# Tap rows by one load, folds evicted in pairs, halved first blocks and last outputs, a new order of pieces

## The chip, the core and the metric

The kernel runs on one core of a Trainium2 chip. A core has a tensor engine (PE, with its weight loads listed as PEld), VectorE (DVE), ScalarE (ACT), GpSimd (POOL) and SyncE (SP), which here issues every DMA. Each engine works through its own queue in order and waits on semaphores for the others. The metric is the device time of the program in microseconds, lower is better; a run gives the time of one whole execution.

## What is computed

Packed attention, then two gated networks, for 8 batches of 576 positions, 8 heads of 64 channels (512 in all):

```python
p_packed = sm_attn(p, k, v)              # 32 packed queries per head
out = sm_attn(q, p_packed, p_packed)     # x = out, heads joined: (8, 576, 512)
gate = sigmoid(conv5(x))                 # causal convolution per channel, 5 taps
val = x @ w_val
x = (gate * val) @ w_out
h = relu(x @ w_in)                       # 1024 wide
u, v = h[..., :512], h[..., 512:]
v_s = w_spatial @ layernorm(v) + b_spatial
return (u * v_s) @ w_out2
```

`w_in`, `w_val`, `w_out`, `w_out2` and the convolution's taps come as 64-bit floats.

## The kernel before

Channels lie on the 128 partitions, positions in the free dimension, so a batch's `x` is four blocks of 128 by 576, worked on in two halves of 288 columns. Products that must keep their precision split both operands into a rounded part `hi` (ScalarE copy) and a rest `lo` (VectorE subtraction), `split` at L137, and take three products of them, `mm3` at L146.

The order of all work is written out by hand: `ORDER` (L21) is a list of tokens, and `run` (L719) advances the generator of each by one step, or by as many as stand behind the dot. `0hv3.2` is two steps of `hv(3)` of batch 0. A step ends at a `yield`, so the list sets each engine's queue. A digit ahead of an attention piece (`sa`, `tr`, `av`, `ppt`, `sb`, `sn`, `sb2`, `m`, `xt`, `cv`) means the batch after it, so that the attention of batch 1 lies among the network of batch 0.

Setup pieces (no digit): `ik`, `ip`, `iv`, `ic` load keys, packed queries, values and taps of batch 0. `ro`, `rw`, `rv`, `ru` (`load_raw`, L583) load a 512-column block of a 64-bit weight, 512 KB; `uo`, `uw`, `uv`, `uu` (`unit`, L588) convert it with `from_f64` (L545): two ScalarE instructions into a temporary, a shift (L554) and an addition (L556) on VectorE. `fv` and `fu` (`fold`, L594) multiply `w_out` with one half of `w_in` into the folded weight `wp`: for each of four 128-row parts `m` four matmuls over `k` (L601), then a ScalarE copy and a VectorE subtraction of 512 columns (L608, L610). Two parts share one accumulator tile. `cb` (`tap_rows`, L651) makes the five taps as rows, repeated for each packed query: a selection matrix on GpSimd, a transpose, five matmuls and two ScalarE copies. `ppk` (L257) multiplies them with the packed values, and `cx` (L352) does batch 0's convolution with them on the tensor engine; the later batches do it in `cv` on VectorE.

Pieces of a batch: `sa` scores of the packed queries with row maxima and exponentials, `av` their weighted values, `ppt` a transpose, `sb` the second scores, `sn` and `sb2` their softmax, `m` the packed values times `w_val`, `xt` the attention output; `val` the gated value `g1`, `hv` the layer-normed half, `hu` the other half, `sp` the spatial product `g2`, `out` (L518) the last product: 2 x 12 matmuls into one accumulator, one ScalarE eviction of 576 columns (L535), one store of 288 KB (L537).

Accumulators come from a pool of four tiles of two banks each (`ps2`, L124); work tiles of 576 columns from a pool of eight (`f`, L113): exponentials, `sn` tiles, convolution sums, gated products before their split, and outputs until their store is done.

Of the kernel before, what the change touches and what calls it, by code (L numbers as in the profile page):

```python
# [21 lines left out]
ik0 ip0 ik1 ic0 cw0.3 cb0 rw0 uw0 sa0 cb0 ro0 sa0 cb0 uw0 uo0.2 rw1 uw1 iv1 cb0 sa0 uw0 uo0 fv3 fv2 sa0 uw1.2 ro1
uo1.3 fv0 ru0 fv1 fv2 iv0 cb0 sa0 tr0 av0 tr1 av1 uu0 rw2 av0 lq0 uu0 uw2 av0 av1 uw2 fv1 av1 ppt0 fv3 uw2 lq1 ppt0
ro2 uu0 ru1 rw3 av0 sb0 fv0 av1 sn1 uo2 lp0 uo2 fu0 sn1 uo2 uu1 sn0 rv2 uu1 sn1 uw3 ro3 sn1 uw3 uu1 sn0 fu1 uw3 ru3
sn0 fv3 uo3.2 uv2 uu3 ru2 fv1 uv2 sb21 fu2 fv0 uo3 uu2 rv0 uu3 fv2 fu1 sn0 sb21 wo0 sb20 fu3.2 fu2 lk1 rv3 uu3 fv0 uv2
uv0 uu2 fv2 uu2 sb21 fv1 sb21 sb20 fv1 sb20.2 rv1 fv1 uv1.2 fv3.2 fv0.2 sb21 uv3 fv3 fu0.2 fu3 fu2 fv2.2 fu3.2 fu0 fu3
wo3 uv1 ws0 fu2 uv3 uv0 sb20 uv3 fu2.2 cx1 uv0 ws3 wo0.2 0lp0 0lq1 sb20 cx1 sb21 fu1 wo0 fu1.2 ws4 m0.2 wo3 m0 cx0 wo3
0val0 wo3 fu1 ws3 lv1 ws1 cx0 fu0.2 0val0 ws3 ws2.2 ws4 0val3.2 0val1.2 0val0.2 0val3 0val2.2 0val0 ws1 0val1.2
0val2.2 lk0 0val1 0val3 0val2 0sa0 0val3 0hv0.2 0sa0 0hv0.2 0sa0 0hv1 ws4 wo0 0hv1.2 0hv0 0sa0 0hu0 0tr0 0hv0.2 ws1
0sa0 0tr1 0hv1 0hv2.2 0hv1.2 0hv2.2 wo3 0hu0 lv0 wo1 0av0.2 wo0 2lp0 0av0 0hv2 0av1.2 wo3 ws2 0hv4 ws0 0hv2.2 wo1 0hv1  # L30
wo1 wo2 0hv3 0hu0 0hv4 0hv3 0av1 0hv4 0hu2 0hv3.2 0hv4.2 0ppt0 0hv4 0ppt0 ws0 0hu2.2 0lq0 0sb0 0sn1 0hv3.2 wo1 0hv4
0hv3 0hu3.2 0sn0.2 0hu1.2 ws4.3 wo1 0sn0 0hv4.2 0sn0 ws4 0sn1.2 0sb20.2 0hv4 0sn1 0sb20.3 0sp2 0sp1.2 wo2 0hu3 0sb21.3
0hu1 0sp1.2 0sp2.2 wo2 0sp0.2 0sb21 0xt0 wo2 0sp0 0sb21.2 0sp1 wo2.2 0sb20 0lv1 0xt0 0sp2.2 0m0.2 0xt1 0m0 0sp0.2
0sp3.3 0xt1 0cv3 1val0.2 0sp3 0cv1 wo1 0sp3 0lk0 0out2 1val1.2 0out2 0cv0 0cv2 0out2 0cv1 0cv2 0out0 0out2 0out0.2
0out1 0cv2 0cv0 0out1.2 0cv3 1val2.2 0out3 0cv1 1val1 0out3 0cv0 1val3 1val2 0cv3 1val3 1val2 1val0.3 1val3 1val1.2
0out1 0lk1 0out3 1val2 1val3 1sa0 1val3 1hv2.2 1sa0.3 1tr0 1hv1.2 1hu3.2 1lq1 1hv0 1sa0 1hv1 1tr1 1hv2 1av1 1hv1 1av1
1hu3 0lv0 1hv2 1av0.2 1av1 1hv1.3 2lq0 1av0 1hv2.2 1hu0.2 1lq0 1hv2 1hv0 1hv3 1hv0 1hv4 1hu0 1hv0.2 1hv3 1hv0.2
1ppt0.2 1hv3.2 1hu1 1hv4.3 1sb0 1hv3.2 1hv4 1m0 1sn0 1hv3 1hu1 1sn0.2 1hu1 1hu2.2 1sn1 1m0 1hv4.3 1m0 1hv4.2 1sp0.2
1sn0 1sb20 1sn1.3 1sb21.3 0out0 1sb21 1hu2 1sb20.2 1sp3.2 1lv0 1sb21.2 1sp3.2 1sp2 1sp0.2 1sp3 1sb20.2 1sp1.3 1sb20
1xt0.2 1sp1 1lk1 1sp2 0out3 1sp2.2 1sp0 1xt1.2 1cv0 2val0 1sp1 2val0 1cv3 1sp2 1out2.2 1cv0 1out2.2 1cv2 1cv3 1lv1  # L40
1out0 1out1.2 1cv0 1cv1 1out3 1out0 1cv3 1out1 1out3.2 1cv1 2val0 2val1.2 2val2 1cv2 1cv1 2val1 1lp0 2val2 2val0.2
2val3.2 1cv2 2val2 2val1 1lk0 2val1 1out0.2 2sa0 2val3 2val2.2 2val3 2lq1 2val3 2hv0 2hv3 2hv0 2sa0.2 2hu1.2 2sa0
2hv0.2 2tr0 2sa0 2tr1 2hv3 2hu1 2hv0.2 2hv3 2hv0 2hu0 2hv2 2hv3.2 2av1.2 2hv3 2av0 2hv3 2hv2.3 2av1 2lv1 2av0.2 2hv1
2ppt0 2hv1.2 2ppt0 2hv1 2hu0 2sb0 2hv2 2sn0 2hv4 2hv2.2 2sn1 2hv4.3 2sn0 2hv1.2 2sn1 2hv4.3 2hu0 2hu2.2 2hv4 2sn1 2hv1
2hu2 2hu3.3 2hv4.2 2sp1.2 2sn0.2 2sp1 2sb20 1out1 2sp0.2 2sb20 2sp1 2lv0 2sb20.2 2sp1 2sn1 2sb21.2 2sp2.2 1out3
2sb21.3 2lk1 2sp0.3 2sb20.2 2sp2.2 2lk0 2sp3.3 2sp2 2xt0.2 2sp3.2 2m0.2 2xt1 2sb21 2xt1 2cv0 2m0 2out1 2cv3 2out1 2cv0
2out1 3val2 2cv2 2cv3 2out2 2out0 2cv1 2out2 3val0.2 2out1 2out2.2 2cv1 3val1 2cv2 2cv0 3val0 3lq1 2out0.2 3val2 2cv3
# [24 lines left out]
6cv1 6sp2 6sp1 6cv1 6sp3 6sp2 6sp3.3 7val2 6sp2 6cv2 6sp3 6cv0 7val0.2 7val2 6cv3 6out1.4 6cv1 6cv2.2 6out3.3 7val1.2
6out2 6cv0.2 7val0 6out2 7val2 7val1 6cv3 6out0.2 7val0.2 7val1 6cv3 7val2 7val1 7val3.3 6out0 7val2 7val3.2 7hv3
6out0 7hv3.4 7hv0 7hv3.2 7hv0.2 7hv1.4 7hv4 7hv1.3 7hv0 7hv4 7hu3.2 7hv4.7 7hv0 7hv2 7hu2 7hu3 7hv0 7hv4 7hv2 7hu2.2
7hu1 7hv2 7hu1.2 7hv2.3 7hu0.3 7hv2 7hv0 7sp0.2 7sp2.2 7sp1 7sp2 7sp3 7sp0.3 7sp2.2 6out2 7sp1.2 7sp3.2 7sp1.2 7sp3.2
6out2 6out3 7out1 7out0.3 7out2 7out1.3 7out3.4 7out0 7out2.3
"""


@with_exitstack  # L80
def packed_attention_gated_mlp(
    ctx: ExitStack,
    tc: tile.TileContext,
    qT: bass.AP,
    kT: bass.AP,
    vT: bass.AP,
    pT: bass.AP,
    w_val: bass.AP,
    conv_w: bass.AP,
    w_outT: bass.AP,  # L90
    w_in: bass.AP,
    wsT: bass.AP,
    w_out2: bass.AP,
    outT: bass.AP,
):
# [35 lines left out]
    def f32(t):  # L131
        return t.bitcast(F32)
# [9 lines left out]
    def mms(out, pairs):  # L142
        for i, (a, b) in enumerate(pairs):
            nc.tensor.matmul(out, lhsT=a, rhs=b, start=(i == 0), stop=(i == len(pairs) - 1))  # L144
# [656 lines left out]
```

## Time and profile before

| | us |
|---|---|
| median of three runs | 587.71 (587.62 to 588.37) |
| the profiled execution | 587.61 |
| its span, first to last instruction | 585.8 |
| tensor engine busy | 570.2 (97%) |
| VectorE busy | 442.8 (76%) |
| ScalarE busy | 298.1 (51%) |

A busy share says how long an engine had an instruction running; where the time could be shorter is read from the engine that the end waits for, stretch by stretch: its timeline with the idle time before an instruction and what ended it, the windows of a batch, and the chain of waits, which is followed back from the last instruction.

### The profile page before, as it was taken

How to read it: one execution, taken by the hardware profiler on the slowest of the kernel's cores; microseconds unless marked ns; L12 is line 12 of the kernel's file. 1: busy time of each engine (PE TensorE's matmuls, PEld its weight loads, DVE VectorE, ACT ScalarE, POOL GpSimd, SP SyncE). 2: the span in 40 equal slices, each digit the busy share in tenths (PEclk: the TensorE clock that was granted, in tenths of full speed). 3: DMA queues.
4: the chain of work that ended last, by engine and by line, in shares of the span. 5: the costliest groups of instructions: out<-in, count | busy, mean ns of one | idle time of the engine just before them, and what ended most of it. 6: DMA issues, size and time to landing. Idle time of an engine off the chain costs nothing.

```text
span 585.8 us, 12443 instructions
## 1 busy us (share of the span) xinstructions
PE 570.2 (97%) x5267; PEld 503.1 (86%) x5267; DVE 442.8 (76%) x847; ACT 298.1 (51%) x524; POOL 27.3 (5%) x51
## 2 busy tenths in 40 slices
PE   3998999999999999999999999999999999999997
PEld 2444889898899989898999989898999899998997
DVE  3697899996879867898759866997779968885330
ACT  4678665654435634654436553655446454453321
POOL 2000010000100010001000010001000010001000
PEclk9999999999999999999999999999999999999999
DMA  8965430053203150023300422013500300000012
GB/s 318 409 268 179 152 107 22 1 194 121 62 1 112 62 204 11 21 67 116 97 1 21 168 90 104 19 49 103 190 24 21 102 2 2 1 20 21 1 41 81
DMA packets 16615, 52.55 MB, mean 90 GB/s; under 512 B 1968, under 2 KB 2992, under 8 KB 16560
## 3 DMA queue, kind: packets, MB, share of 16 engines
q1 hardware_dynamic: 16560, 51.77, 25.0%
q8 instruction: 41, 0.67, 0.5%
q14 instruction: 14, 0.11, 0.1%
HBM read 42.32 MB, written 9.44 MB: 88 GB/s over the span
## 4 chain that ended last, share of the span: by engine, by line
PE 93%; DVE 4%; DMA 1%; ACT 1%; issue 0%; SPq 0%; DVEq 0%; ACTq 0%
PE ps L144 82%; PE ps L601 2%; PE ps L238 2%; PE ps L194 2%; PE ps L341 2%; PE ps L273 2%; PE ps L325 1%; DMA kq<-kT 1%; PE ps L360 1%; DVE wp L610 1%; DVE sT L286 0%; DVE sT L306 0%; DVE mx L202 0%; DVE sm L301 0%; DVE raw L556 0%
## 5 line engine op out<-in xcount | busy, mean ns | idle before, releaser
L144 PE MATMUL ps<-ws,vn 128*128 128x288 f32 (+1 forms) x896 | 122.1, 295 | 0.0
L144 PEld LDWEIGHTS ps<-ws,vn 128*128 128x128 f32 (+1 forms) x896 | 119.6, 188 | 2.4 <-issue 1.3
L144 PEld LDWEIGHTS ps<-g,wp 128*128 128x128 f32 x768 | 103.5, 188 | 5.0 <-issue 3.2
L144 PE MATMUL ps<-g,wp 128*128 128x288 f32 x768 | 107.3, 296 | 0.0
L144 PE MATMUL ps<-g,wo 128*128 128x288 f32 x768 | 105.9, 295 | 1.0 <-DVE g L140 1.0
L144 PEld LDWEIGHTS ps<-g,wo 128*128 128x128 f32 x768 | 102.9, 188 | 3.0 <-ACT x L349 1.3
L380 DVE SCALAR_TENSOR_TENSOR acc<-x,cw,acc 128x572 f32<-128x572 f32 (+1 forms) x112 | 90.0, 815 | 4.3 <-ACT acc L376 1.0
L144 PE MATMUL ps<-wp,g 128*128 128x512 f32 x384 | 91.9, 393 | 0.0
L144 PEld LDWEIGHTS ps<-wp,g 128*128 128x128 f32 x384 | 70.8, 188 | 16.5 <-issue 0.7
L138 ACT CAST g<-g 128x576 fp32r<-128x576 f32 x64 | 42.4, 675 | 56.7 <-DVE g L510 40.8
L140 DVE TENSOR_TENSOR g<-g,g 128x576 fp32r<-128x576 f32 x64 | 47.7, 751 | 6.5 <-ACT g L138 5.7
L457 POOL TENSOR_TENSOR rstd<-rstd,mhalf 128x1 f32<-128x1 f32 (+1 forms) x40 | 23.6, 593 | 522.2 <-DVE rstd L455 447.6
L138 ACT CAST vn<-vr 128x512 fp32r<-128x512 f32 (+1 forms) x40 | 24.6, 622 | 45.1 <-DVE vr L459 45.0
L510 DVE TENSOR_TENSOR g<-ps,u 128x576 f32<-128x576 f32 x32 | 23.8, 753 | 27.4 <-PE ps L144 26.9
L535 ACT COPY o<-ps 128x576 f32<-128x576 f32 x32 | 20.3, 635 | 35.7 <-PE ps L144 35.7
L144 PE MATMUL ps<-Ah,Mh 128*128 128x288 f32 x128 | 37.9, 296 | 0.0
L144 PE MATMUL ps<-Ah,Ml 128*128 128x288 f32 x128 | 37.8, 295 | 0.0
L144 PE MATMUL ps<-Al,Mh 128*128 128x288 f32 x128 | 37.8, 295 | 0.0
L439 ACT ACTIVATE vr<-ps 128x512 f32<-128x512 f32 x32 | 19.2, 602 | 34.9 <-PE ps L144 32.3
L140 DVE TENSOR_TENSOR vn<-vr,vn 128x512 fp32r<-128x512 f32 (+1 forms) x40 | 27.0, 684 | 13.1 <-ACT vn L138 12.9
L451 DVE BATCH_NORM_STATS2 st<-vr 128x6 f32<-128x512 f32 (+1 forms) x40 | 27.4, 685 | 11.7 <-ACT vr L439 9.0
L459 DVE TENSOR_SCALAR vr<-vr,mv,rstd 128x512 f32<-128x512 f32 (+1 forms) x40 | 21.2, 536 | 11.9 <-POOL rstd L457 11.8
(108 smaller groups left out, 680.4 us busy)
## 6 DMA issues: line engine op xcount, KB each, us to landing
v<-vT SPq DMA_DIRECT2D x16, 650.0 KB, 5.0
kq<-kT SPq DMA_DIRECT2D x16, 576.0 KB, 4.7
kq<-qT SPq DMA_DIRECT2D x16, 576.0 KB, 4.3
outT<-o SPq DMA_DIRECT2D x32, 288.0 KB, 2.5
raw<-w_in SPq DMA_DIRECT2D x8, 512.0 KB, 10.4
raw<-w_outT SPq DMA_DIRECT2D x4, 512.0 KB, 9.9
raw<-w_val SPq DMA_DIRECT2D x4, 512.0 KB, 10.3
raw<-w_out SPq DMA_DIRECT2D x4, 512.0 KB, 7.6
```

The lines of the kernel that those rows point to most:

```text
L138: nc.scalar.copy(out=hi, in_=src)
L140: nc.vector.tensor_tensor(out=lo, in0=src, in1=f32(hi), op=ALU.subtract)
L144: nc.tensor.matmul(out, lhsT=a, rhs=b, start=(i == 0), stop=(i == len(pairs) - 1))
L194: nc.tensor.matmul(ps[g][NPK * qt:NPK * qt + NPK, h // 2, SQ * (h % 2):SQ * (h % 2) + SQ], lhsT=pT_, rhs=k[:, SQ * qt:SQ * qt + SQ], start ...
L238: nc.tensor.matmul(ps[NPK * h:NPK * h + NPK, :65], lhsT=aT[:, 9 * (h // 2) + 4 * (h % 2) + t, :], rhs=v[:, h, t, :], start=(t == 0), stop= ...
L380: nc.vector.scalar_tensor_tensor(out=acc[:, sft:], in0=x[:, :S - sft], scalar=cw[:, c, tap:tap + 1], in1=acc[:, sft:], op0=ALU.mult, op1=A ...
L439: nc.scalar.activation(out=vr, in_=ps, func=AF.Relu)
L451: nc.vector.bn_stats(st[:w], vr[:w])
L457: nc.gpsimd.tensor_tensor(out=rstd[:w], in0=rstd[:w], in1=mhalf[:w], op=ALU.pow)
L459: nc.vector.tensor_scalar(out=vr[:w], in0=vr[:w], scalar1=mv[:w, 0:1], scalar2=rstd[:w], op0=ALU.subtract, op1=ALU.mult,)
L510: nc.vector.tensor_tensor(out=halves(t), in0=ps[:, :, :SH], in1=halves(self.u.pop(c)), op=ALU.mult)
L535: nc.scalar.copy(out=halves(t), in_=ps[:, :, :SH])
```

## The change

- `ORDER` is a new list for the setup and all batches. The first weights that are loaded and folded are now the `u` half of `w_in` and `w_out`, then the `w` half; taps (`ic`, `cb`) come later.
- `FIRST`: the blocks `o0` and `w0` are loaded and converted in two column halves.
- `fold(j, hf)` takes two parts `m` at once, matmuls alternating between the two banks of one tile, and evicts both with one copy and one subtraction of 1024 columns.
- `tap_rows` loads the rows already repeated (`conv_r`, 128 x 640 values of 64 bit, made by the host) and converts them; the selection matrix, the transpose and the matmuls go.
- In the last batch (`cut`) the matmuls of `hv`, `hu`, `sp` and `out` are cut into steps of three, and `out` evicts and stores each half of 288 columns by itself, with an accumulator of its own for the second.
- `sa` may stop between its head pairs; the dictionaries of loaded tiles are read without removing the entry.

```diff
-ik0 ip0 ik1 ic0 cw0.3 cb0 rw0 uw0 sa0 cb0 ro0 sa0 cb0 uw0 uo0.2 rw1 uw1 iv1 cb0 sa0 uw0 uo0 fv3 fv2 sa0 uw1.2 ro1
...
-6out2 6out3 7out1 7out0.3 7out2 7out1.3 7out3.4 7out0 7out2.3
+ip0 ik0 ik1 ro0 uo0 sa0.4 uo0 ru0 ro0 uu0.3 uo0 fu0 iv0 ru1 iv1 uo0.3 sa0 tr0 sa0 tr1 fu1 av0.2 uu1 av1 uu1 ro1 lq1
+lq0 av0 uu1 fu0 uo1 fu1 uo1 av1.2 uo1 ppt0.2 rw0 uw0 rw0 uw0 fu1 sb0 uw0.2 fu0.2 uw0 fu1 sn0 uw0 sn1 fv1 sn0 rw1 uw1
+rw2 uw1 sn1 uw2 uw1 sn1 uw2 sn0 ro2 uo2 fv0 fv1 uo2 rw3 uw2 sn1 fv0 sb21 fv0 ro3 uo2 sn0 sb20 sb21 fv1.2 uo3.2 fv0 ru2
+uw3.2 sb20 fv1.2 fv0.2 uu2 ic0 uu2 uw3 uo3 fv1 uu2 cb0.3 sb21 ru3 uu3 cb0 uu3 lp0 sb20 fv1.2 av1 av0 uu3 rv0 uv0 fv0.2
+fu1 rv3 uv3 sb20 fv0 rv2 fu1 fv1 sb21 ws2 fv0 uv0 fu1.2 ws4 ws3 fu0.2 uv3 uv2 rv1 uv1 sb20 sb21 wo0 uv1 cx0 uv2 2lp0
+ws1 uv0 lv0 uv1 uv2 uv3 fu1.2 fu0.2 sb21 wo0.2 cx0 lk1 m0 cx1 sb20 m0 wo0 fu0 m0 0val0.2 fu0 0val2.2 ws3.2 cw0.2 cx1
...
+7sp2 7sp3.2 6out2 7sp3.5 7sp1 7out1 7out0 7sp2 7sp1.2 7out0 7sp2 7sp3 7out1 7out0 7out3.2 7out2.2 7sp3 7out2 6out1
+7sp3 7out0 7out1.2 7out2 7out3 7out0 7out3 7out1.3 7out0.2 7out2.2 7out3 7out1.2 7out0.2 7out3 7out2.3 7out3.3
...
+    def mms(out, n, pair, cut=False):
+        for i in range(n):
+            a, b = pair(i)
+            nc.tensor.matmul(out, lhsT=a, rhs=b, start=(i == 0), stop=(i == n - 1))
+            if cut and i % 3 == 2 and i < n - 1:
+                yield
...
+            for n in range(2):
+                if self.cut and n:
+                    ps = ps2.tile([P, 2, 512], F32, tag="ps2", name="ps2")
...
+                if self.cut:
+                    nc.scalar.copy(out=t[:, ss], in_=ps[:, n, :SH])
+                    nc.sync.dma_start(out=dst[:, ss], in_=t[:, ss])
...
+    def parts(kind, k):
+        return [slice(0, DM // 2), slice(DM // 2, DM)] if kind + str(k) in FIRST else [slice(0, DM)]
...
+    def fold(j, hf):
+        ps = ps2.tile([P, 2, 512], F32, tag="ps2", name="ps2")
         hs = slice(hf * DM, (hf + 1) * DM)
         for k in range(NC):
+            for i in range(2):
+                m = 2 * j + i
+                nc.tensor.matmul(
+                    ps[:, i], lhsT=woT[:, k, P * m:P * m + P], rhs=homes["uw"[hf]](k),
+                    start=(k == 0), stop=(k == NC - 1),
+                )
+                yield
...
+        hi, lo = (w[:, 2 * j:2 * j + 2, hs] for w in wp)
+        yield from split(hi, lo, ps)
...
     def tap_rows():
...
+        n = CONV * P
+        block = vn_p.tile([P, 4 * n], I32, tag="vn1", name="taps")
+        raw, tmp = block[:, :2 * n].rearrange("p (n t) -> p n t", t=2), block[:, 2 * n:]
+        nc.sync.dma_start(out=raw, in_=words(conv_r))
+        yield
+        dst = block[:, :n]
+        cwr.append(dst.bitcast(F32).rearrange("p (a b) -> p a b", a=CONV))
+        yield from from_f64(lambda: dst, raw, n, tmp=tmp)
```

## Rows read from the trace of the kernel before

**Rows 1.** From the page: engine totals, then granted clock and traffic in 40 slices.

```profile
PE 570.2 (97%) x5267; PEld 503.1 (86%) x5267; DVE 442.8 (76%) x847; ACT 298.1 (51%) x524; POOL 27.3 (5%) x51
...
PEclk9999999999999999999999999999999999999999
...
GB/s 318 409 268 179 152 107 22 1 194 121 62 1 112 62 204 11 21 67 116 97 1 21 168 90 104 19 49 103 190 24 21 102 2 2 1 20 21 1 41 81
```

**Rows 2.** Windows of two batches: stretch, length, busy time per engine (instructions), clock, DMA.

```profile
195.20:261.52 66.32, 66.32 (x642) 60.54 (x647) 52.22 (x100) 33.33 (x58) 3.21 (x5) 1.00 0.23 79
...
327.88:394.45 66.57, 66.57 (x642) 60.59 (x648) 53.21 (x101) 32.67 (x57) 3.11 (x5) 1.00 0.24 82
```

**Rows 3.** Timeline of the tensor engine, setup: start, length, instruction, idle before and releaser.

```profile
14.04 6.75 PE L601 MATMUL ps<-winv,woT 128*128 128x512 f32 x10 [1.67 <-DVE woT L556]
...
46.67 1.12 PE L601 MATMUL ps<-raw,woT 128*128 128x512 f32 x2 [1.85 <-DVE wp L610]
...
55.86 0.40 PE L144 MATMUL ps<-Ah,Mh 128*128 128x288 f32 x1
```

**Rows 4.** Timeline of the weight loads around the change of their distance.

```profile
17.62 0.34 PEld L601 LDWEIGHTS ps<-winv,woT 128*128 128x128 f32 x1 [0.52 <-issue]
18.47 0.20 PEld L601 LDWEIGHTS ps<-winv,woT 128*128 128x128 f32 x1 [0.52 <-issue]
18.91 0.19 PEld L601 LDWEIGHTS ps<-winv,woT 128*128 128x128 f32 x1 [0.24 <-issue]
```

**Rows 5.** Chain that ended last, pieces of the setup: start, length, what.

```profile
1.64 5.92 DMA kq<-kT
...
20.79 1.29 PE ps L238 x78
...
24.34 1.24 PE ps L273 x32
...
47.79 2.61 PE ps L360 x80
...
52.32 1.02 PE ps L325 x16
```

**Rows 6.** Timeline of the end of the run, all engines.

```profile
567.72 0.69 PE L144 MATMUL ps<-g,wo 128*128 128x288 f32 x4
567.92 0.76 DVE L510 TENSOR_TENSOR g<-ps,u 128x576 f32<-128x576 f32 x1 [1.11 <-PE ps L144]
...
569.40 12.50 PE L144 MATMUL ps<-g,wo 128*128 128x288 f32 x92 [0.99 <-DVE g L140]
...
582.00 0.64 ACT L535 COPY o<-ps 128x576 f32<-128x576 f32 x1 [0.96 <-PE ps L144]
```

**Rows 7.** Timeline of VectorE, setup.

```profile
8.90 1.42 DVE L202 TENSOR_REDUCE mx<-ps 128x4 f32<-128x576 f32 x2 [0.37 <-PE ps L194]
10.36 0.68 DVE L208 COPY m<-mx 32x8 f32<-32x8 f32 x4
...
11.75 0.19 DVE L211 TENSOR_REDUCE m<-m 32x8 f32<-32x32 f32 x1
11.97 0.69 DVE L214 TENSOR_SCALAR nb<-m 32x8 f32<-32x8 f32 x4
...
13.30 0.69 DVE L556 CUSTOM_DVE_ANT_0 woT<-woT,tmp 128x1024 uint16<-128x1024 uint16 x1
13.90 0.42 DVE L554 TENSOR_SCALAR winv<-tmp 128x512 int32<-128x512 int32 x1
...
54.54 1.23 DVE L140 TENSOR_TENSOR Ml<-ps,Mh 128x1024 fp32r<-128x1024 f32 x1 [2.53 <-ACT Mh L138]
...
58.19 0.69 DVE L610 TENSOR_TENSOR wp<-ps,wp 128x512 fp32r<-128x512 f32 x1 [0.65 <-ACT wp L608]
```

**Rows 8.** DMA issues of the last 3.5 us: count, KB each, us to landing.

```profile
outT<-o SPq DMA_DIRECT2D x1, 288.0 KB, 2.1
```

**Rows 9.** Groups by line and form, first 80 us: busy time, mean ns of one.

```profile
L369 ACT ACTIVATE gate<-ps 128x288 f32<-128x288 f32 x8 | 2.6, 422 | 0.0
```

More of the change, by code (lines that the diff above doesn't have):

```diff
@@ L20 @@
 GATE0 = True
+FIRST = ("o0", "w0")
 ORDER = """
[L22 to L25 removed]
@@ L26 @@
[L26 to L35, printed above, removed]
@@ L140, in split, with mm3, pair @@
         nc.vector.tensor_tensor(out=lo, in0=src, in1=f32(hi), op=ALU.subtract)
-    def mms(out, pairs):
-        for i, (a, b) in enumerate(pairs):
-            nc.tensor.matmul(out, lhsT=a, rhs=b, start=(i == 0), stop=(i == len(pairs) - 1))
-    def mm3(out, steps):
-        mms(out, [p for (ah, al), (bh, bl) in steps for p in ((ah, bh), (ah, bl), (al, bh))])
+    def mms(out, n, pair, cut=False):
[4 more added lines that the diff above has]
+                yield
+    def mm3(out, n, step, cut=False):
+        def pair(i):
+            (ah, al), (bh, bl) = step(i // 3)
+            return ((ah, bh), (ah, bl), (al, bh))[i % 3]
+        return mms(out, 3 * n, pair, cut)
     vn = []
@@ L179, in __init__, with scores, head @@
             self.pp = self.ppk = self.x = None
-        def heads(self, lhsT, kind):
-            src = [kq_t.pop((kind, self.b, i)) for i in range(2)]
-            return [ps2.tile([P, 2, 512], F32, tag="ps2", name="ps2") for _ in range(2)], [
-                (g, h, lhsT[64 * g:64 * g + 64, NPK * h:NPK * h + NPK], src[h // 2][64 * g:64 * g + 64, h % 2])
-                for h in range(4)
+        def scores(self):
+            return [ps2.tile([P, 2, 512], F32, tag="ps2", name="ps2") for _ in range(2)]
+        def head(self, lhsT, kind, h):
+            src = kq_t[kind, self.b, h // 2]
+            return [
+                (g, lhsT[64 * g:64 * g + 64, NPK * h:NPK * h + NPK], src[64 * g:64 * g + 64, h % 2])
                 for g in range(2)
@@ L189, in sa @@
         def sa(self, _):
-            ps, heads = self.heads(pbd_t.pop(self.b), "k")
-            for i in range(0, 8, 2):
+            ps = self.scores()
+            for h in range(4):
                 for qt in range(4):
-                    for g, h, pT_, k in heads[i:i + 2]:
+                    for g, pT_, k in self.head(pbd_t[self.b], "k", h):
                         nc.tensor.matmul(
@@ L269, in sb @@
         def sb(self, _):
-            ps, heads = self.heads(self.ppT, "q")
+            ps = self.scores()
             for n in range(2):
-                for g, h, pT_, q in heads:
-                    nc.tensor.matmul(
-                        ps[g][NPK * h:NPK * h + NPK, n, :SH],
-                        lhsT=pT_, rhs=q[:, n * SH:(n + 1) * SH],
-                        start=True, stop=True, tile_position=(64 * g, NPK * h),
-                    )
+                for h in range(4):
+                    for g, pT_, q in self.head(self.ppT, "q", h):
+                        nc.tensor.matmul(
+                            ps[g][NPK * h:NPK * h + NPK, n, :SH],
+                            lhsT=pT_, rhs=q[:, n * SH:(n + 1) * SH],
+                            start=True, stop=True, tile_position=(64 * g, NPK * h),
+                        )
             self.sps = ps
@@ L400, in val @@
                 ss = slice(n * SH, (n + 1) * SH)
-                mm3(
-                    ps[:, n, :SH],
-                    [
-                        ((at.M[0][:, g, cs], at.M[1][:, g, cs]), (at.A[g][0][:, ss], at.A[g][1][:, ss]))
-                        for g in range(2)
-                    ],
+                yield from mm3(
+                    ps[:, n, :SH], 2,
+                    lambda g: ((at.M[0][:, g, cs], at.M[1][:, g, cs]), (at.A[g][0][:, ss], at.A[g][1][:, ss])),
                 )
@@ L432, in hv @@
             w_hi, w_lo = ([w[:, k, DM:] for k in range(NC)] for w in wp)
-            g1 = [self.g1[k] for k in range(NC)]
             ts_ = slice(P * tt, P * tt + w)
             if w == P:
-                mm3(ps, [((g1[k][:, 0, ts_], g1[k][:, 1, ts_]), (w_hi[k], w_lo[k])) for k in range(NC)])
+                yield from mm3(
+                    ps, NC, lambda k: ((self.g1[k][:, 0, ts_], self.g1[k][:, 1, ts_]), (w_hi[k], w_lo[k])), self.cut
+                )
                 yield
@@ L440, in hv @@
             else:
-                mms(ps, [(self.tail[:, k, :], wk) for k in range(NC) for wk in (w_hi[k], w_lo[k])])
+                yield from mms(ps, 2 * NC, lambda i: (self.tail[:, i // 2, :], (w_hi, w_lo)[i % 2][i // 2]))
                 yield
@@ L475, in hu @@
                 ss = slice(n * SH, (n + 1) * SH)
-                mm3(
-                    ps[:, n, :SH],
-                    [
-                        (
-                            (wp[0][:, k, cs], wp[1][:, k, cs]),
-                            (self.g1[k][:, 0, ss], self.g1[k][:, 1, ss]),
-                        )
-                        for k in range(NC)
-                    ],
+                yield from mm3(
+                    ps[:, n, :SH], NC,
+                    lambda k: ((wp[0][:, k, cs], wp[1][:, k, cs]), (self.g1[k][:, 0, ss], self.g1[k][:, 1, ss])),
+                    self.cut,
                 )
@@ L692, in packed_attention_gated_mlp @@
         "uu": lambda k: unit("u", k),
-        "fv": lambda m: fold(m, 1),
-        "fu": lambda m: fold(m, 0),
+        "fv": lambda j: fold(j, 1),
+        "fu": lambda j: fold(j, 0),
         "ws": spatial,
@@ L770, in by_pair @@
         return np.moveaxis(w, 0, axis)
+    conv = rows(by_pair(inputs["moe_conv_w"].T, 0)).transpose(1, 0, 2)
     wt, bias = inputs["moe2_w_spatial"].T, inputs["moe2_b_spatial"]
@@ L783 @@
         "w_val": rows(by_pair(by_pair(inputs["moe_w_val"], 0), 1)),
-        "conv_w": rows(by_pair(inputs["moe_conv_w"].T, 0)).reshape(128, -1),
+        "conv_w": conv.transpose(1, 0, 2).reshape(128, -1),
+        "conv_r": np.repeat(conv.transpose(0, 2, 1).reshape(4, -1), NPK, axis=0),
         "w_outT": rows(by_pair(inputs["moe_w_out"], 0).T),
```

196 lines of the change are left out of this document (86 added, 110 removed).

## Prediction

> **What bounds the kernel now.** I read the engine totals first [rows 1]: the tensor engine is busy for 97% of the span, VectorE for 76%, ScalarE for 51%. So the question is where the other 3% lies, and whether the matmuls themselves change. The windows of single batches answer the second half [rows 2]: in a batch of about 66.3 us the tensor engine has no idle time at all, while VectorE is busy for 52 to 53 us and ScalarE for 33. Of six batches the best took 66.32 us and the worst 66.57; together they hold some 0.5 us that another order could win. A batch keeps its matmuls and their shapes, so the middle of the kernel can hardly get faster; it can only lose.
>
> What is left are the two ends. At the start the reader should follow the tensor engine's timeline [rows 3]: the first fold matmul starts at 14.04, after waiting for VectorE, a gap of 1.85 us opens before 46.67 because a fold accumulator isn't evicted yet, and the first `val` matmul, from which on everything is dense, starts at 55.86. The work in between is known: 32 fold matmuls of two passes, 0.43 us a pass at the full clock [rows 4], are 27.5 us; `av` 1.3, `ppt` 0.1, `sb` 1.2, `m` 1.0 and two `cx` of 2.6 make 8.8 [rows 5]; 36.3 us in all. But 55.86 - 14.04 = 41.8. Of the 5.5 us too many, 1.85 is that gap, 2.2 the slow beginning (below), and the other 1.4 lies in many short waits. At the end of the run [rows 6] the tensor engine comes to the outputs, does four matmuls from 567.72 (0.134 us each, so until about 568.26) and then stands until 569.40, 1.15 us, because the fourth `g2` tile is still going through VectorE, ScalarE and VectorE. Then the last eviction (0.64 us) and the last store follow.
>
> **The first fold matmul.** Before, it waits for two whole blocks, `winv` and `woT`. Their conversion stands in VectorE's queue around the row maxima of the scores: 1.42 + 0.68 + 0.19 + 0.69 us for these, 0.42 and 0.69 for each block, from 8.90 to 13.99 [rows 7]. After, it needs one whole block (`u0`) and one half (`o0`, 256 columns): the same 3.0 us of maxima from 8.90, to about 11.95, then a shift of 0.25 (a little over half of 0.42), 0.42, 0.69 and 0.37, less the overlap: start at about 13.6, 0.45 us earlier. The data are there: the second key block lands 5.9 us after its issue at 1.64 [rows 5], with 256 KB and then 512 KB behind it in the queue, 0.64 and 1.28 us at its 409 GB/s [rows 1]; so 8.2 and 9.5 us. The bounds are 0 (the maxima decide anyway) and 1.1 us (one block's 0.42 + 0.69 saved whole).
>
> **The tap rows.** A transpose, five matmuls, two ScalarE copies and two GpSimd instructions go. They lay ahead of 14.04, where the tensor engine waits for VectorE anyway, so they give nothing. In their place come 640 KB by DMA, 1.6 us of a queue that is full in the second slice of the page and over half full in the third [rows 1], two ScalarE instructions, and on VectorE a shift and an addition of 640 columns, by the rows of 512 columns 0.5 and 0.85 us. That is a real charge, since VectorE is the second busiest engine; and `ppk` (0.85 us) moves behind it, after the scores `sb`. GpSimd's memsets of `vn` move behind the last use of the taps' block, to about 40 us; they are first read in batch 0, and GpSimd is idle at 95% [rows 1].
>
> **The folds.** Eight ScalarE copies and eight subtractions of 0.69 us become four and four of 1024 columns. A subtraction of that size is in the trace, 1.23 us [rows 7]: 4 x 1.23 = 4.9 in place of 8 x 0.69 = 5.5 us, 0.6 less, about half of what the taps add.
>
> **The setup, followed by hand.** With these durations (VectorE's next instruction starts some 0.08 us before the one ahead has had its full time, as 13.30 and 13.90 show) I put the new order on the engines. The tensor engine: folds from 13.6 with the slow beginning; a wait of about 0.6 before `ppt`, as the `av1` steps now stand in VectorE's queue behind a shift that waits for ScalarE; `sb` ends at 23.4, as against 25.6 before [rows 5]. From there VectorE has 29 us in one queue up to the subtraction `Ml`, without which `val` can't go on: 12.4 block conversions in place of 11, the taps and `ppk` among them. ScalarE, with two instructions a block, makes it wait once, about 1.0 us, before the shifts of `uv1` and `uv2`, and `m` then waits some 0.7 us for `fu1` to be evicted. `Ml` ends at about 53.4; the tensor engine for its part comes to 13.6 + 36.3 + 2.2 + 0.6 + 0.7 = 53.4. The two meet, so `val` starts at 53.5 to 53.8 instead of 55.86: **2.1 us gained**. The fold evictions now lie under the matmuls of the other folds; without that cover the 1.85 us come back. The bounds: if nothing waits, 13.6 + 36.3 + 2.2 = 52.1, a gain of 3.7; if VectorE's queue is 2 us later than I have it, 0.
>
> **The slow beginning.** Weight loads of the folds are 0.85 us apart up to 18.47 and 0.43 from then on [rows 4], although the page gives the granted clock as full throughout [rows 1]: the first five passes ran at the lower of the two levels (1.2 and 2.4 GHz), after a time in which the tensor engine had mostly waited, and cost 5 x 0.43 = 2.2 us. After, it has no tap matmuls between the scores and the folds and stands from about 8.9 to 13.6; I keep the 2.2 us, since in both cases folds and `av` then follow without a break. The Trainium skill, TensorE: Matmul & The Clock Gate, Part 1, says that the half clock is the state of rest, that continued work lifts it and that pauses bring it back. The five passes agree, and by it a start with more pauses would stay slow for longer (rival 3).
>
> **The middle.** The instructions of batches 0 to 6 stay; what moves are places in the queues. Two things I counted along the two orders. The switches between exponential and sigmoid on ScalarE are 16 in both. The eight work buffers `f` are fuller: after, all eight are taken nine times, before, once, because several stores (`1out2`, `0out3`, `3out0`) stand in SP's queue two or three batches after their eviction, among loads. An instruction on VectorE or ScalarE that needs a buffer then waits for a store to land, 2.1 us [rows 8], and behind it stand evictions that free accumulators for the tensor engine. With VectorE idle for 13 of 66 us and ScalarE for 33 [rows 2] I put this at 0; the bounds are -0.5 (the excess of the worse batches) and +5.
>
> **The last batch.** After, `hv`, `hu`, `sp` and `out` of batch 7 come in pieces of three matmuls, and the outputs begin with `g2[0]` and `g2[1]`. Behind the last `sp` matmul I count 30 output matmuls before the first one that needs the last `g2`, 4.0 us; the chain behind `sp3` took 1.48 us, from 567.92 to 569.40 [rows 6], and has one more subtraction and one wait ahead of it, about 2.7. So the 1.15 us vanish; the other bound is 0. Inside the batch `sp` now reaches `vn2` some 4.8 us after `hv2`, whose normalisation is a chain over three engines; I take it as just covered.
>
> **The very end.** The last eviction is of 288 columns, not 576; the nearest row, a ScalarE instruction on 288 columns out of PSUM, has 0.42 [rows 9], 0.22 less than 0.64. The store falls from 288 to 144 KB. The trace gives 2.1 us for 288 KB [rows 8] and nothing for 144; it can't save more than the time of the bytes, 0.36 us at 409 GB/s, and need not save any, with eight stores in place of four: I take 0.3. The Trainium skill, DMA: Bandwidth & Descriptors, Anatomy of one DMA, gives a fixed 2.0 us and the bytes at 436 GB/s, fitted on another issuing path: 2.7 us for 288 KB, where the trace has 2.1. The saving by it would be an estimated 0.34, and the sum the same.
>
> **The sum.** The profiled execution took 587.61 us (span 585.8 and 1.8 around it); the median of the runs is 0.1 above. 2.1 (start) + 1.15 (last outputs) + 0.5 (eviction and store) = 3.75 from 587.61 is **583.9**.
>
> **Rivals.**
> 1. The setup gains nothing: VectorE's queue behind `sb`, longer by 1.35 of taps, 0.85 of `ppk` and 1.6 of conversions, becomes the bound, and `val` starts at 55.8 again. For it: these 3.8 us. Against it: `sb` is 2.2 us earlier, and VectorE had free time before. Only the end wins: 586.0.
> 2. Slower: the full `f` buffers. Place: VectorE and ScalarE in batches 3 to 7, nine points; price: up to a store's 2.1 us each, of which the tensor engine sees what the accumulators don't cover. From 0.55 us a point it makes the kernel measurably slower; at 0.7 us the time is 590.2. Against it: the idle shares of both engines.
> 3. The lower clock lasts until the `fv` folds: 9.4 us of work up to about 25.9 would take 7.2 us longer, of which 1.3 hide waits: 589.8. For it: a longer pause before 13.6. Against it: in the kernel before the clock rose within 4.4 us of continued folds.
> 4. Everything fits: start 3.7, last outputs 1.15, end 0.6, middle 0.5: 581.7.
>
> **How the numbers follow.** Forecast 0.52 (583.0 to 585.0), rival 1 0.20, rival 2 0.10, rival 3 0.06, rival 4 0.12. The range, 581.4 to 587.4, takes in rivals 1 and 4 and what lies between them and no change; it leaves out 2 and 3. A measurement of this kernel can tell about 0.2%, 1.2 us. Faster by more than that: 0.52 + 0.12 + 0.14 of rival 1 = 0.78; within it: 0.06 of rival 1 and 0.02 of rival 2 = 0.08; slower: 0.08 + 0.06 = 0.14.
>
> **What would show it.** Right: first fold matmul at 13.3 to 13.9; no wait of the tensor engine for `wp` any more; first `val` near 53.6; batches of 66.3 to 66.6 us; no wait at the outputs; last eviction 0.42 and its store under 2.1 us. Wrong: fold weight loads 0.85 us apart beyond 19 us, batches of 67 us in which VectorE or ScalarE wait for stores, or `val` waiting for `Ml` after 55 us.

## The result and the profile after

| | before | after |
|---|---|---|
| median, us | 587.66 | 582.62 (582.33 to 583.15) |
| the profiled execution | 587.61 | 582.79 |
| its span | 585.8 | 581.0 |
| tensor engine busy | 570.2 (97%) | 566.9 (98%) |
| VectorE busy | 442.8 (76%) | 445.0 (77%) |
| ScalarE busy | 298.1 (51%) | 299.2 (52%) |

The ratio of after to before is 0.9913, with an interval of 0.9896 to 0.9931: 5.0 us faster. The forecast was 583.9 in a range of 581.4 to 587.4.

Where the 4.8 us of the spans come from is read by putting the tensor engine's landmarks of both traces side by side:

| stretch | before | after | won |
|---|---|---|---|
| start to first fold matmul | 14.04 | 12.81 | 1.23 |
| first fold to first `val` (55.86, 52.38) | 41.82 | 39.57 | 2.25 |
| `val` to the scores of batch 7 (460.9, 458.15) | 405.0 | 405.8 | -0.8 |
| from there to the last matmul's end | 121.0 | 119.6 | 1.4 |
| last matmul's end to the end of the span | 3.9 | 3.25 | 0.65 |

The tensor engine's timeline of the kernel after, setup, answers [rows 3] and [rows 4] (start, length, instruction, idle before and what ended it):

```profile
5.33 2.54 PE L207 MATMUL ps<-kq,pbd 64*32 64x144 f32 x64 [5.33 <-DMA kq<-kT]
12.81 3.78 PE L614 MATMUL ps<-raw,woT 128*128 128x512 f32 x4 [4.95 <-DVE woT L565]
16.52 1.48 PE L252 MATMUL ps<-v,aT 128*32 128x65 f32 x80
17.94 1.98 PE L614 MATMUL ps<-raw,woT 128*128 128x512 f32 x4
20.12 0.30 PE L278 MATMUL ps<-ident,pp 128*128 128x128 f32 x1 [0.20 <-ACT pp L266]
```

Behind the first fold the only wait that the timeline names is the 0.20 before `ppt`. The 1.85 us wait for `wp` is gone. The first four fold passes are still 0.85 us apart, as their weight loads show:

```profile
13.83 0.34 PEld L614 LDWEIGHTS ps<-raw,woT 128*128 128x128 f32 x1 [0.52 <-DVE woT L565]
14.68 0.34 PEld L614 LDWEIGHTS ps<-raw,woT 128*128 128x128 f32 x1 [0.52 <-issue]
```

`ps<-v,aT` is `av`, and after it the passes come every 0.43.

The chains that ended last, from the start to the first row maximum, say why the first fold is so much earlier. Of after:

```profile
1.64 4.96 DMA kq<-kT
6.65 1.32 PE ps L207 x32
7.97 1.42 DVE mx L216 x2
```

In [rows 5] the same load has 5.92 us. The second key block lands 0.96 us earlier, and everything on VectorE up to the first fold moves with it.

The windows of three batches of after (columns as in [rows 2]) show the middle; the last row is batch 0 of before:

```profile
58.95:125.88 66.93, 66.78 (x635) 60.81 (x634) 60.24 (x114) 38.70 (x69) 3.11 (x5) 1.00 0.25 86
192.29:258.69 66.40, 66.40 (x635) 60.54 (x634) 52.85 (x100) 33.59 (x59) 3.54 (x5) 1.00 0.24 82
391.42:458.15 66.73, 66.62 (x635) 60.59 (x634) 53.44 (x101) 33.39 (x58) 3.43 (x5) 1.00 0.25 84
...
62.43:128.79 66.36, 66.36 (x635) 60.69 (x634) 60.14 (x114) 41.44 (x72) 3.36 (x5) 1.00 0.25 90
```

Batch 0, the first row, takes 66.93 us where it took 66.36. The sixth window, the third row, takes 66.73 where it took 66.49; the others are within 0.25 us of theirs, one of them shorter. The timeline of the end answers [rows 6]:

```profile
564.88 12.88 PE L149 MATMUL ps<-g,wo 128*128 128x288 f32 x96
...
566.94 0.76 DVE L144 TENSOR_TENSOR g<-g,g 128x576 fp32r<-128x576 f32 x1 [0.74 <-ACT g L142]
...
577.79 0.40 ACT L540 COPY o<-ps 128x288 f32<-128x288 f32 x1 [0.40 <-PE ps L149]
```

All 96 output matmuls run in one row. The last `g2` is ready at 567.70, 2.8 us after the first of them, and the thirty that don't need it last 4.0.

### The profile page after: what moved, and what is told of

Its sections match the earlier page's. It is cut to its first block, busy times and chain, and to the rows that moved or that the text cites. A ratio compares the mean times of both kernels' runs of the same rounds, so it can differ in the third digit from the quotient of the medians.

```text
span 581.0 us, 12435 instructions
## 1 busy us (share of the span) xinstructions
PE 566.9 (98%) x5256; PEld 501.5 (86%) x5256; DVE 445.0 (77%) x849; ACT 299.2 (52%) x528; POOL 26.8 (5%) x49
## 3 DMA queue, kind: packets, MB, share of 16 engines
q1 hardware_dynamic: 17568, 52.42, 25.3%
## 4 chain that ended last, share of the span: by engine, by line
PE 94%; DVE 3%; DMA 1%; ACT 1%; issue 0%; POOL 0%; SPq 0%; POOLq 0%; ACTq 0%
PE ps L149 81%; PE ps L614 5%; PE ps L207 2%; PE ps L356 2%; PE ps L252 2%; PE ps L288 1%; PE ps L340 1%; PE ps L375 1%; DMA kq<-kT 1%; DVE vn L144 0%; DVE st L465 0%; DVE vr L473 0%; DVE sT L306 0%; DVE sT L301 0%; POOL rstd L471 0%
## 5 line engine op out<-in xcount | busy, mean ns | idle before, releaser
L149 PEld LDWEIGHTS ps<-g,wp 128*128 128x128 f32 x768 | 105.2, 188 | 5.1 <-issue 2.8
L149 PE MATMUL ps<-g,wp 128*128 128x288 f32 x768 | 109.4, 296 | 0.0
L149 PE MATMUL ps<-wp,g 128*128 128x512 f32 x384 | 93.8, 395 | 0.0
L498 ACT ACTIVATE u<-ps 128x576 f32<-128x576 f32 x32 | 20.7, 650 | 22.3 <-PE ps L149 22.1
```

The lines of the kernel that those rows point to most:

```text
L498: nc.scalar.activation(out=halves(u), in_=ps[:, :, :SH], func=AF.Relu)
```

## Experiments

"Middle" means from batch 0's first network piece to batch 7's. First fold and first `val` are times in the profiled execution.

| run | median, us | ratio to before, interval | first fold | first `val` |
|---|---|---|---|---|
| after | 582.62 | 0.9913 (0.9896 to 0.9931) | 12.81 | 52.38 |
| setup_alone | 584.19 | 0.9939 (0.9923 to 0.9954) | 12.73 | 52.62 |
| setup_tail | 581.93 | 0.9903 (0.9886 to 0.9921) | 12.85 | 52.23 |
| tail_whole | 585.25 | 0.9958 (0.9943 to 0.9973) | 12.69 | 52.58 |
| taps_early | 583.27 | 0.9922 (0.9907 to 0.9937) | 12.96 | 52.89 |
| keys_first | 584.16 | 0.9941 (0.9923 to 0.9958) | 13.87 | 53.84 |
| whole_block | 583.25 | 0.9928 (0.9911 to 0.9945) | 13.32 | 53.15 |
| whole_outputs | 583.22 | 0.9924 (0.9909 to 0.9940) | 12.80 | 52.18 |
| fold_single | 583.13 | 0.9922 (0.9904 to 0.9940) | 12.79 | 52.94 |
| stores_behind | 585.89 | 0.9986 (0.9960 to 1.0012) | 12.77 | 52.42 |
| evict_first | 582.80 | 0.9917 (0.9902 to 0.9932) | 12.75 | 52.57 |
| taps_matmul | 582.37 | 0.9911 (0.9892 to 0.9930) | 12.86 | 52.43 |
| maxima_split | 581.46 | 0.9896 (0.9881 to 0.9910) | 12.21 | 51.90 |

The intervals are some 2 us wide, as wide as most steps. So the medians say little about 0.5 us, and the verdicts below rest on the stage times of the profiles.

**setup_alone, setup_tail, tail_whole: the three stretches by themselves.** Their edit is a splice of the two lists in `ORDER`, with the steps already done left out; `setup_alone` and `tail_whole` also have

```diff
-            self.cut = at.b == B - 1
+            self.cut = False
```

> The changed kernel up to the first network piece of batch 0 (with its halved first blocks, tap rows by DMA, paired folds), and from there the order of the kernel before, with its tail: whole pieces in the last batch, whole last outputs. Computes the same. Theory (the three gains add up and stand where the profiles show them: 3.48 us at the first val, minus 0.76 in the middle, 1.43 at the last batch's pieces, 0.65 behind the last matmul): the first val starts at 52.4, every batch from then on takes its time of before (66.32 to 66.57), and the whole is 587.7 - 3.5 = 584.2 us. Rival (the order of the kernel before fits only its own setup, and gives the gain back in batch 0): first val at 52.4, but batch 0 takes 67 us or more and the whole is 585.0 to 586.5. My prediction's own term for the setup (2.1) would give 585.6 with the first val at 53.5 to 53.8.

Measured 584.19, with batches of 66.32 to 66.55, each as before, and the 0.99 us wait at the outputs back. The theory holds: the gain of the setup stays whole.

> The changed kernel up to the first network piece of batch 0 and from the first network piece of batch 7 on; between them the order of the kernel before. Computes the same. Theory (the 0.76 us that the middle lost are of the new order of pieces there, above all of batch 0, where the wave hv4, hv3, hv1 leaves no free accumulator at 80.46): batch 0 takes 66.4 instead of 66.92, batch 6's 0.60 wait at 407.8 is gone, and the whole is 582.6 - 0.7 = 581.9 us. Rival (batch 0 loses because the shorter setup leaves more conversions over for it, so that any order is late there): batch 0 stays at 66.8 to 67.0 and the whole at 582.5.

Measured 581.93; batch 0 in one window:

```profile
58.79:125.14 66.35, 66.35 (x635) 60.70 (x634) 59.84 (x114) 40.02 (x70) 3.37 (x5) 1.00 0.24 83
```

With the same setup and the old order batch 0 has no idle time. So its 0.57 us are of the new order of pieces, not of the shorter setup. The sixth window takes 66.47 again, too, so the 0.24 lost there are of the order as well. What in that order costs batch 0 its time is the question of evict_first.

> The changed kernel up to the first network piece of batch 7; the last batch in the order of the kernel before, with its pieces uncut (12 or 14 matmuls to a step) and whole last outputs. Computes the same. Theory: the 1.43 us between batch 6's sa and the last matmul and the 0.65 us behind it come back: 582.6 + 2.1 = 584.7 us, with the waits of the kernel before in front of the last outputs (about 1 us) seen again. My prediction's terms (1.15 + 0.5) would give 584.3. Rival (the order alone, or the uncut pieces with free accumulators, would do as well): 582.6 to 583.2.

Measured 585.25, with 121.24 us from the scores of batch 7 to the last matmul (after: 119.60) and 3.72 behind it (3.25): 2.1 us in the stages, as the theory has it. The remaining 0.2 of the spans' 2.3 is the later `val`, the 0.3 up to the medians is their spread. The wait is back in the tensor engine's timeline:

```profile
567.08 12.50 PE L146 MATMUL ps<-g,wo 128*128 128x288 f32 x92 [0.99 <-DVE g L141]
```

**taps_early, keys_first: why the second key block is early.** Two lists that differ from after's in one place each:

```diff
-ip0 ik0 ik1 ro0 uo0
+ip0 ik0 ik1 ic0 ro0 uo0     (taps_early; the later ic0 goes)
+ik0 ip0 ik1 ro0 uo0         (keys_first)
```

> One DMA is moved: the load of the 20 tap columns (128 rows of 160 bytes) stands right behind the two key blocks, as in the kernel before, instead of some 20 us later. Computes the same. Theory (its small rows hold up the key blocks that are still under way, which is why the second key block landed at 6.60 us and not at 7.56): second key block at about 7.5, row maxima 0.9 later, first fold at about 13.7 instead of 12.8, first val at 53.3, the whole 583.5 us. Rival (the key block is early for another reason, the packed queries going first): it lands at 6.6 as before this edit, first fold at 12.8, the whole stays at 582.6.

> The first two loads change places: key block 0, packed queries, key block 1, as in the kernel before; all else as in the changed kernel. Computes the same. Theory (it is this place of the packed queries that holds the second key block up): the first scores start earlier, at about 4.9, but wait for the second key block, which lands at 7.5; row maxima start 0.9 later, first fold at about 13.7 instead of 12.8, first val at 53.3, the whole 583.5 us. Rival (the second key block is early because 256 KB stand behind it in place of a whole block, or for a reason outside the order of loads): it lands at 6.6, first fold 12.8, the whole 582.6.

The theory of taps_early falls: its second scores start at 6.80 after a wait of 0.34 (6.69 and 0.29 in setup_tail, which has the loads of after), the first fold at 12.96. Its median, 583.27, looks like the theory's 583.5, but `av` took 0.4 us longer in its profile than in that of after, and most of the 0.5 us by which `val` is later is that. The one of keys_first holds. Its tensor engine's timeline at the start:

```profile
4.98 1.21 PE L207 MATMUL ps<-kq,pbd 64*32 64x144 f32 x32 [4.98 <-DMA pbd<-pT]
7.71 1.22 PE L207 MATMUL ps<-kq,pbd 64*32 64x144 f32 x32 [1.52 <-DMA kq<-kT]
13.87 3.78 PE L614 MATMUL ps<-raw,woT 128*128 128x512 f32 x4 [4.95 <-DVE woT L565]
```

The 64 KB of packed queries between the two key blocks land after 3.7 us instead of 1.8, and the second key block, issued at the same time as in after (1.63), comes later: the second scores start at 7.71 instead of 6.65. With this one exchange of two loads the first fold is 1.06 us later, nearly all that it had won. (`val` is 0.5 later than expected, again by a slow `av`.) What the transfers do to each other inside the DMA engines no run here shows.

**whole_block, fold_single, taps_matmul: the parts that the change names.**

```diff
-FIRST = ("o0", "w0")
+FIRST = ()                               (whole_block)

-        yield from split(hi, lo, ps)
+        for i in range(2):               (fold_single)
+            nc.scalar.copy(out=hi[:, i], in_=ps[:, i])
+        yield
+        for i in range(2):
+            nc.vector.tensor_tensor(out=lo[:, i], in0=ps[:, i], in1=f32(hi[:, i]), op=ALU.subtract)

-ip0 ik0 ik1 ro0 uo0 sa0.4 uo0 ru0        (taps_matmul, with tap_rows of before)
+ip0 ik0 ik1 ic0 ro0 cw0.3 cb0 uo0 sa0.2 cb0.2 sa0 cb0 sa0 uo0 ru0
```

> The first blocks of both weights are loaded and converted whole (one load of 512 KB, one shift and one addition of 512 columns in place of two halves each); all else as in the changed kernel. Computes the same. Theory (the half takes 0.42 - 0.29 of the shift and 0.69 - 0.42 of the addition off VectorE's way to the first fold): row maxima still at 7.95, first fold at 13.2 instead of 12.8, first val 0.2 to 0.4 later, the whole 582.9. Rival A (the 512 KB behind the keys hold up the second key block): it lands at 7.5, first fold at 14.0 or later, the whole 583.8. Rival B (the halves cost VectorE as much later as they save first): first fold 13.2, first val as before this edit, the whole 582.6.

Its maxima start at 7.89 and its first fold at 13.32: the halves are worth 0.5 us there, and they stay up to `val`. The theory holds, and rival A falls. Its terms give only 0.40, though. The rest is at least in part a wait of VectorE: `u0` now stands behind 512 KB instead of 256, ScalarE begins to convert it at 10.26 instead of 9.40, and VectorE, through with the shift of `o0` at 11.44, starts that of `u0` only at 11.51.

> Each fold of two parts is evicted by two ScalarE copies and two VectorE subtractions of 512 columns, at the places where one copy and one subtraction of 1024 columns stand; all else as in the changed kernel. Computes the same. Theory (the pairing takes a fixed part off each instruction: 2 x 0.69 - 1.23 = 0.15 us a fold on VectorE, 0.6 us in all, hidden beside the folds): first fold 12.8, the subtraction Ml 0.2 to 0.6 later and the first val at 52.4 to 52.9, the whole 582.6 to 583.0. Rival (the pairing of the evictions is what removed the 1.85 us wait for wp): a wait of the tensor engine for wp or an accumulator opens again, first val after 53.3, the whole 583.6 or more.

From `cx0` to `val` it takes 8.44 us where all other kernels with the new setup take 8.24 to 8.29. No wait for `wp` opens. So pairing the evictions is worth 0.16 us. The rest of its later `val` is the slow `av` described below. What took the 1.85 us away is then the new order, in which the evictions lie under other folds' matmuls. That is argued by elimination: no run puts the old order of the folds back.

> The tap rows are made as in the kernel before (20 tap columns loaded behind the keys, a selection matrix, a transpose, five matmuls, two ScalarE copies) inside the new setup, in place of the 640 KB load and its conversion; all else as in the changed kernel. Computes the same. Theory (the matmuls lie ahead of the first fold, where the tensor engine waits anyway, and VectorE is spared 0.5 + 0.8 us later): first fold at 12.8 to 13.1, the wait for VectorE at Ml shorter, first val at 51.9 to 52.6, the whole 582.2 to 582.8; that would mean that the repeating DMA brought nothing by itself. Rival (the small tap load and its steps on three engines hold the row maxima and the first fold up): first fold at 13.3 or later, first val at 53 or later, the whole 583.3 or more.

First fold at 12.86, first `val` at 52.43, 582.37. The matmuls fit into the wait for VectorE:

```profile
7.85 0.39 PE L674 MATMUL ps<-ident,cw 128*20 128x128 f32 x1
9.19 2.46 PE L681 MATMUL ps<-cwt,sel 20*128 20x128 f32 x10 [0.96 <-ACT cwt L677]
12.86 1.22 PE L615 MATMUL ps<-raw,woT 128*128 128x512 f32 x1 [1.21 <-DVE woT L566]
```

The repeating DMA by itself brings nothing, as the theory had it. Nor do the 1.3 us of VectorE that it adds cost anything.

**whole_outputs: the very end.** Accumulator, eviction and store of an output in one, the steps of three kept:

```diff
-                if self.cut:
-                    nc.scalar.copy(out=t[:, ss], in_=ps[:, n, :SH])
-                    nc.sync.dma_start(out=dst[:, ss], in_=t[:, ss])
...
+            nc.scalar.copy(out=halves(t), in_=ps[:, :, :SH])
+            if not self.cut:
+                yield
+            nc.sync.dma_start(out=dst, in_=t)
```

> The last batch's outputs are evicted and stored whole again (one accumulator, one ScalarE copy of 576 columns, one store of 288 KB each); the order and the steps of three matmuls stay. Computes the same. Theory (terms of the very end): last matmul ends at 577.8 as before this edit, the last eviction takes 0.64 instead of 0.40 and the store 0.3 more, so the tail behind the last matmul is 3.7 to 3.8 us instead of 3.2 and the whole 583.1 to 583.2. Rival (eight small stores cost what they save, or the second accumulator of each output is what lets the matmuls run through): tail unchanged and 582.6, or a gap of the tensor engine among the outputs and 583.5 or more.

Its last eviction:

```profile
577.44 0.64 ACT L537 COPY o<-ps 128x576 f32<-128x576 f32 x1 [0.16 <-PE ps L149]
```

The tail behind the last matmul is 3.79 us (after: 3.25), of which 0.24 is the eviction (0.64, 0.40) and 0.3 the store (2.1 us for 288 KB, 1.8 for 144). No gap opens among the outputs. The theory holds.

**stores_behind: the late stores.** In the list every fourth step of an `out` of batches 0 to 6 (the store) moves right behind the third (the eviction):

> In the changed kernel every store of the outputs of batches 0 to 6 is issued right behind its eviction instead of up to three batches later; nothing else moves. Computes the same. Theory (full buffers f cost nothing, since VectorE and ScalarE are ahead of the tensor engine): batches 1 to 5 stay at 66.3 to 66.7 us, the whole at 582.6 within 0.2 us. Rival (my rival 2: instructions that need a buffer wait for late stores, with a price the tensor engine partly sees): batches 0 and 6, the two long ones, lose 0.3 to 0.5 us each, the whole 581.8 to 582.2. A third way (the stores now collide with loads in the queue): one batch longer by 0.5 us or more.

Measured 585.89, two thirds of the gain lost (one of its runs, of 590.35, pulls its ratio up). The batches take 66.90, 66.39, 66.37, **67.57**, **68.16** and 66.73 us (each counted from the scores of the batch that follows it). SP's timeline ahead of batch 4's scores, first of stores_behind, then of after:

```profile
243.53 12.58 SPq L544 DMA_DIRECT2D outT<-o  x4
256.20 0.38 SPq L167 DMA_DIRECT2D kq<-kT  x1
```

```profile
249.90 0.34 SPq L545 DMA_DIRECT2D outT<-o  x1
250.36 0.37 SPq L168 DMA_DIRECT2D kq<-kT  x1
```

Four stores that wait for their evictions stand in front of the key load, so it is issued at 256.20 instead of 250.36, and 4.1 us later the tensor engine is still waiting for it:

```profile
260.37 0.73 PE L206 MATMUL ps<-kq,pbd 64*32 64x144 f32 x32 [0.99 <-DMA kq<-kT]
...
328.61 0.73 PE L206 MATMUL ps<-kq,pbd 64*32 64x144 f32 x32 [1.66 <-DMA kq<-kT]
```

Between 230 and 400 us SP waited for evictions 117.9 us in 12 waits, in after 71.8 in 3. The Trainium skill, DMA: Bandwidth & Descriptors, Anatomy of one DMA, says, of another issuing path, that a semaphore wait is held by the issuing sequencer ahead of the dispatch, while the DMA engines only empty their queues. The trace agrees: the load was late by its issue, not by its transfer. So the third way came true, and the theory's time falls with it. Its reason stands: the four batches in which no load is late take within 0.03 us the same as in after, with stores early or late (66.93, 66.41, 66.40 and 66.73 there), so the full `f` buffers of my rival 2 cost nothing in them. What the late stores do is keep the loads' way free, and after's order is worth some 3 us against this one.

**evict_first: batch 0.** One place of the list:

```diff
-0hv4 wo2 0hu1 0hv4 0ppt0 0hv4 0hv0 0hv3.2 ws1
+0hv4 wo2 0hv0 0hu1 0hv4 0ppt0 0hv3.2 0hv4 ws1
```

> In batch 0 of the changed kernel two steps move in front of two others: VectorE's subtraction that ends hv0 goes ahead of the normalisation of hv4 (which waits for GpSimd until 78.5), so that its buffer is free earlier, and hv3's ScalarE eviction goes ahead of hv4's copy, which waits for that normalisation. Computes the same. Theory (this wait is what keeps hv3's accumulator and holds hv1's matmuls up by 0.92 us at 80.46): the eviction at 79.81 comes about 1 us earlier, the gap goes, batch 0 takes 66.3 to 66.5 us instead of 66.92, the whole 582.1. Rival (the normalised tiles that sp needs come late whatever frees the accumulator): the gap moves to the front of sp at about 89.7, batch 0 stays at 66.8 or more, the whole 582.6.

The eviction of `hv3` starts at 78.99 instead of 79.81, as meant, and batch 0 takes 66.90: nothing won. The weight loads still stand idle there, now up to `hv4`'s copy, which the edit put off from 79.15 to 79.91. First after, then evict_first:

```profile
80.46 2.60 PEld L149 LDWEIGHTS ps<-wp,g 128*128 128x128 f32 x12 [0.92 <-ACT vr L453]
...
80.53 2.63 PEld L149 LDWEIGHTS ps<-wp,g 128*128 128x128 f32 x12 [0.84 <-ACT vn L142]
```

So the edit put one wait in the place of another. The theory falls all the same, because these are rows of the weight loads, which stand idle while matmuls run; I had read them as rows of the matmuls. Those of `m` start at 79.38 in after and the next ones 1.08 us later, in evict_first 1.00 us later (79.53 to 80.53), and behind the `m` of the setup it is 1.02 (48.61 to 49.63). Less than 0.1 us can have been lost there. The wait that the tensor engine's own row does show in batch 0 is the rival's; in evict_first:

```profile
90.79 4.38 PE L149 MATMUL ps<-ws,vn 128*128 128x288 f32 x31 [0.19 <-DVE vn L144]
```

Five `sp` matmuls start from 89.78 on at 0.13 us each, so the sixth was due at about 90.4 and comes at 90.79: 0.35 of the 0.57 us, waiting for the last normalised tile, whose subtraction VectorE ends at 90.73. (In after the weight loads wait for the same subtraction, up to 90.63.) The other 0.2 us are in waits too short for the timeline; they stay open.

**maxima_split: a faster kernel.** From setup_tail, one place more:

```diff
-ip0 ik0 ik1 ro0 uo0 sa0.4 uo0 ru0 ro0 uu0.3 uo0 fu0
+ip0 ik0 ik1 ro0 uo0 sa0.3 uo0 ru0 ro0 uu0.3 uo0 sa0 fu0
```

> Starts from the kernel of setup_tail (the changed setup and tail, the middle of before; 581.93 us). On VectorE the conversions that the first fold needs go between the two halves of the row maxima's work instead of behind it. Computes the same. Theory (the start is bound by VectorE's queue from 7.9 on): first fold at 12.1 instead of 12.8, the exponentials 1.2 us later, which the fold passes cover but for 0.3, first val 0.3 to 0.5 earlier, the whole 581.5. Rival (behind sb VectorE's queue up to Ml decides, and its work is the same): first fold at 12.1 but first val where it was, 52.2, the whole 581.9; or av late by more than was won, 582.3.

First fold at 12.21, first `val` at 51.90, 581.46 (581.25 to 581.54), 6.1 us under before and below both kernels; the runs of setup_tail took 581.77 to 582.32. The theory holds; of the 0.64 us that the first fold won over setup_tail, 0.33 reach `val`, because `av` took 1.47 us in this run and 1.19 in setup_tail's.

## Why the prediction was right, and which terms were off

The sign and the places were right; the sum was 1.3 us short. The median lies below the forecast's own 583.0 to 585.0. The two ends came out as rival 4 had them (3.48 of its 3.7 at the start, 1.4 and 0.65 of its 1.15 and 0.6 at the end), and only the middle, which lost 0.8 instead of winning 0.5, keeps the time above its 581.7. So the sum was as near as it was in part by luck: the start gave 1.4 us more than I had, and the middle took 0.8 of it back. Of the signs, the missing waits at `wp` and at the outputs and the size of the last eviction and store came true; the first fold (12.81, not 13.3 to 13.9), the first `val` (52.38, not 53.6) and two of the batches (66.93 and 66.73) did not. Step by step:

- **First fold, 0.45 predicted, 1.23 measured.** The failed step is "the second key block lands 5.9 us after its issue". I carried the duration of before over to a list in which the two loads ahead of it had changed places. keys_first gives the price, 1.06 us. From the first row maximum to the first fold it is 4.86 us (7.95 to 12.81) in place of 5.14 [rows 3, 7], so 0.28 won there against my 0.45; by whole_block it is the halves that win it. My upper bound of 1.1 was built on VectorE's work alone and was too low for the same reason.
- **The tap rows.** The queue's room and the place behind `sb` were right, and the matmuls "give nothing" is shown by taps_matmul. The "real charge" on VectorE isn't one.
- **The setup behind the first fold, 39.8 predicted, 39.57 measured.** The size was right by two errors that cancel. The waits of 0.6 before `ppt` and 0.7 at `m` were 0.20 and none. But the 1.4 us of short waits that I saw in the kernel before, and let vanish, are still there: 36.3 of work, 1.7 of four slow passes and 0.2 make 38.2. From `sb` to `cx0` the time is 22.78 or 22.79 us in every kernel here with the new setup. The tensor engine decides there, not VectorE: taps_matmul, with 1.3 us less on VectorE, has the same 22.79, and in after `Ml` is done at 52.14, while the tensor engine's `cx1` runs to 52.4. Rival 1 falls.
- **The slow beginning, 2.2 predicted.** Four passes instead of five, 1.7 us, and in part `av` (below). Rival 3 falls.
- **The middle, 0 predicted, 0.8 lost.** Within the bounds (-0.5 to +5) and by a mechanism I hadn't named: the order of pieces, by setup_tail, of which 0.35 us is the wait for the last normalised tile in batch 0. Rival 2 falls: batches 3 and 4 of after, two of those that it named, take 66.40 and 66.33 us, and stores_behind won nothing.
- **Last outputs, 1.15 predicted, 1.4 measured.** The wait vanished with 1.2 us to spare. The chain behind the last `sp` took 2.82 us, by my count 2.7. The 0.3 more are smaller waits, which no run took apart; one that before has in its last batch is that of the weight loads for `g1` at 529.79 (0.40, in after 0.19 at most).
- **The very end, 0.5 predicted, 0.65 measured.** The eviction gave 0.24 (0.22 predicted), the store 0.3 (0.3).

## What to carry to other kernels

When a change reorders loads, don't carry a load's duration over from the old order: ask what stands in front of it in the queue. Here a small load that is needed together with two large ones did better ahead of them than between them, by 1.06 us at the first fold. A store that waited for its data held up the loads behind it on the same queue, so such a store is better put late, behind the loads. And before a gap is explained, look whether it is the matmuls or only the weight loads that stand idle.

## What the runs showed of the hardware beyond that

With the granted clock given as full throughout [rows 1], the tensor engine doubles its rate in each run with the new setup within or close to `av`, after four fold passes 0.85 us apart. That place wanders between executions: in seven kernels with the same setup (after, setup_alone, setup_tail, tail_whole, whole_outputs, stores_behind, evict_first) the weight loads of `av` took 1.19 to 1.98 us, and the first `val` came 52.18 to 52.62 accordingly. The order is the same in both: the two with 1.19 have 52.18 and 52.23, the one with 1.98 has 52.62. So some 0.4 us of the place of the first `val` goes with the time at which the higher of the two levels (1.2 and 2.4 GHz) comes, as the distance of the passes shows it and the granted clock of the page doesn't. A later `val` in one profile, as in fold_single (2.15 us), must be cleared of it first.
